# Another common order, engine choices and PSUM banks for the same operations in a four-block attention kernel

## The chip, the cores and the metric

The kernel runs on one core of a Trainium2 chip. The metric is the device time of one execution in microseconds (us), taken as the median of several runs. Before the change it is 410.13 us.

## The reference

Four residual blocks follow each other on an input `x` of 2048 tokens by 512 features, in bfloat16, two of kind A (linear attention) and two of kind B (attention to the last 256 tokens), all with 32 heads of 16 features:

```python
def _A_ref(x, wqkv, wo):
    ...
    phi = lambda t: jnp.where(t > 0, t + 1, jnp.exp(t)) + 1e-6
    pq, pk = phi(q), phi(k)
    kv = jnp.einsum("bhsd,bhse->bhde", pk, v)
    z = jnp.einsum("bhsd->bhd", pk)
    num = jnp.einsum("bhqd,bhde->bhqe", pq, kv)
    den = jnp.einsum("bhqd,bhd->bhq", pq, z)[..., None] + 1e-6
    o = num / den
    return (...) @ wo

def _B_ref(x, wqkv, wo):
    ...
    mask = (idx[:, None] - idx[None, :] >= 0) & (idx[:, None] - idx[None, :] < W)
    p = _softmax(jnp.where(mask, scores, -1e9), axis=-1)
    o = jnp.einsum("bhqk,bhkd->bhqd", p, v)
    return (...) @ wo

x = x + _A_ref(_layernorm(x), A_wqkv, A_wo)
x = x + _B_ref(_layernorm(x), B_wqkv, B_wo)
x = x + _A_ref(_layernorm(x), A_wqkv, A_wo)
x = x + _B_ref(_layernorm(x), B_wqkv, B_wo)
```

## The kernel before

The tokens are cut into 16 tiles of 128. The residual stream stays in SBUF (`xres`) throughout. The class `Plan` first writes down some 2,500 operations as a graph, each with the engines it may run on, what it reads and writes, and the PSUM tiles it uses. Nothing is scheduled on the chip: `place()` unpacks a table of bytes, `TABLE`, and takes four things from it: one common order of all operations, the engine of each, the PSUM bank (one of eight) of each PSUM tile, and which of an operation's waits stands first. Each engine then runs its operations in that common order, and `synchronise()` adds the semaphore waits that data and banks need. A PSUM bank goes to its next tile only when all users of the tile before are done, so the banks set waits too.

The work falls into three stretches:

- **Keys of the first A block** (to about 50 us). For each tile: mean and variance of the row (`stats` L382, `aggr` L383 on DVE), a power on POOL (`pow` L384), the normalised row (`xn` L385), a transpose (L391 by DMA, or L397 on PE with a copy L404), key and query projections (L420, L434), and `phi` from an exponential on ACT (L443) and VectorE work (L444, L448, L450). Sums over tokens gather in PSUM (L501).
- **First middle stretch** (about 50 to 250 us): for each token tile the end of block A, block B, and the keys, queries and values of the second A block. Denominators of the A block come for four tiles together: a matmul group `den` (L563), a reciprocal (L567), its copy `recb` (L568), a spreading matmul group `spread` (L576), and one multiply per tile, `pqd` (L583 on DVE), after which `aout` (L420, `ps<-M,XQ`) multiplies by the folded output weights and `res` (L594) adds to the residual.
- **Second middle stretch** (about 250 to 409 us): the same A end and B block for the last two blocks.

Inside block B, for a token tile `j`: projections of queries and keys `bq` and `bk` (L434, `ps<-xT,wBp`, 16 matmuls a tile each) and values `bv` (L420, `ps<-wBv,xT`); copies out of PSUM `bqe` and `bve` (L409) and `bke` (ACT L615 or DVE L616), each on ACT or DVE as the table says; two DMAs from SP for the keys (`kd`, L624, `kB<-vp`) and two for the values (`vd`, L643), which rearrange them. Then score matmuls `s` (L667, and L709 or L712 for the far edge), exponentials `ex` on ACT (L677 and L722), masks on DVE or POOL (`mk`, L687 or L686, and L736 or L733; `mf`, L745 or L744), products with the values `pv` and `pw` (L768, L780), a reciprocal and a multiply on DVE (`rcp` L790, `div` L791), a DMA transpose `oT` (L391, `oT<-o`), the output projection `bout` (L420, `ps<-wBo,oT`), and again `res` (L594). In the second stretch rows of the result go out by a DMA from SP or POOL (L891). The staging area of the keys is cleared beforehand by ACT (L863) or POOL (L861).

The reading of the table, in `place()`:

```python
    order = [ops[raw[2 * k] + 256 * raw[2 * k + 1]] for k in range(n)]
    ...
        o.eng = ("PE", "ACT", "DVE", "POOL", "SP")[raw[2 * n + o.i]]
    ...
        x.banks = [raw[3 * n + k]]
    ...
        o.first = raw[3 * n + len(tiles) + o.i]
```

Of the kernel before, what the change touches and what calls it, by code (L numbers as in the profile page):

```python
# [900 lines left out]


TABLE = (
    r"c-p;M1-Kly&b4Gow!_TK%*@Qp%*@Qp%*@Qp%*@Qp427iJf99rrZQ3O7Chhy@?(WRm($Ue8?3v9MRMAxoRZvA%g;W#;N~x&osY|O0t8^;8DxzYlqN<pB<}#=!",
# [3 lines left out]
    r"N)ddm%BuD%GYnPL)E#wN?NVn|Lsd?7R2>w<H|n0s0-e;iDufa!3hkl1Dyb5~8)YB~M1bn>Ksm4w1d2gv^;VTpXH-&123a9F)PQUd5hB45RYBcXVN?qEUIl~V",
    r"Fib^;C=eA&KuL%Or64=xfbUdJ$OSQ=1Js0CP#S7OP>2pGp$yc8+)x(kKs~4r%^{Qur<y?{6;^eGRFDTcLpi9f8bC|v11+GU>I*AWD`*XEV5Mpc{a~u<1QFCU",
    r"wMwl~tJPYyTZL3zpesyQGgUX}4l~p&)dTjZ{?HS8!8tVm210K*ubQYqa6!$3`LGHGLtV817D9bhPpyVEP+MJ6d({D01a(w+6&%*WR@esXpoUru4b&3Yr!K04",  # L910
    r"@KCLXnyQw1q?STswO?(35b%Rq1_#u3xU8PSHCPUh)pghbPt=cU4n$H<)e1NSH((<?Q#&Cf?1IA(3XZ^0_(=_cl`s^Zfx=(ZEeH+6U@q*2O#pZko&(}=*bF1!",
    r"Hr#>Jum?uN7GOLB$6zFkf{5xBoQ1n!Q1Au3hTwP{_QF2+3PR%7a34ZoD0~SI;34dX(AWlJLR)+UVbEbLI0uA3tFU+vEC#`7*bcvepr|n%K7r`?Ewsm9RTPYh",
    r"9q<IafnfL}#D?<_2TsB%hzmbK42+FM@G)F~)c7;R#5h<Kb7L_qj<GNgUW5Xe2K!(kEQoKRBj&}vm=;T5VJwN4U<~Ai?;sz<#qXgL_QO(G8uLRLjE7^P9HxdJ",
    r"pa2wvvX~Fc<1Y{&6JQ$XjA>yY4#ujO5UXK2sE+BO2G+zxH~<IXNF0rq;aA9pS6~R%!CF`w>tc8uh5a!CX2<S02CqUy?14G3Cl1BLm;_0)u7~MxIPS&tI1Dpj",
    r"B#ew>aUYJyao7+VL4FjyACuw;%!rMlJ~qG!SOF_yCQOFOu?aMVF4z?t;tZ^WhcE>m!I^j%yWuoEiqml%q{LL13v=Qz?2RXI7S6`GI0p~lJlughu?il?@sJs_",
    r";4VCfli?IjfJsmpv*Kx7i|cSAoWbk39yj1Qyn*GR7gm68@LOzz8}TH*!LxWCH{k`mh!r8YzKJ1qV+^62U?r#wx3DSR#yfZy!|Tm>4<qVdQRxVJK019Lw_s3h",
    r"bu&z_gXj!;0fJtL8TBHZh*MxHgwmaL7d;6>>#aB$w_zk5R(I78a4{~y{Q44x(FJrcJr%d(6ugWD^;?Xg!|5w{6*K9Wx`Z}5mX59C==l0OjH~xxNnJ$8)7P++",
    r"PM`<tqI!rfrpxH1_z;KcY4AP%fRFGo?#AZW0?X>+x}2_{3+r6EB|gEYsC6r>sas=tom<z^c{J*Ty0q@5pJ63kQIF7>b!A;!*U`)HM;xw4=`p&l&Z4vGk-C8{",
    r"q{rz*I<c;&8|wNxi5{zy>d5*hjH-XeDEc{$*2^)v?x%mj2|AnZuP5r``h*^!8|f)JnO=b_agv^<PwM2lyH26A>odBCo~(1|srsyLtjFsnI;U=`qv`4ToPL3;",
    r"aIT)Go9Ui9pI(g@bYA@uFX@Z=yl$>v;e35aFVHD<3%v$g>MDAnKCEA3Rs9uK(_iBfy;P^ty>x1QMK98e^)TIA_t9x|XgZ>=>8m=ePN%0s80xEM!VNtGs_U>+",  # L920
    r"Lod@ebt?@t3uXh-cCBfko}q8)9eSr;u2<+;dZpf_@95q7wqB(l>PLE}zN_cx{4_{Mp?i9d-m7Qp0(4y;)vI+>YOUMoXcUZsQ$dPAA?UHbtlR3-Iubq6Pjx%p",
    r"UdNz_RGyycHTr>$NiXzEeM*O?3Uo|A*KsHoRiwxik783?8caiIC?%&VL=>G;P<%>C$tWc;6{3B*8r7hxl#0?&O`1$oC^hZZ;pml4OSPy0HKNKSG?g0C0sUHk",
    r"r45CobaYVHp|5pyDn;MuZ}l4;ib~U3U6<-neQHUCsR+%WS=5TslcizQnAYiWG@fSCeO-n!&;*)8Z*?Vd6oiJ;TpB?cDJa#ZqV%1fN0}%y6{9SafLc=<YD*m`",
    r"5iOyFw2azOR%%ZjX(?^dTlF@*UeBkIG@CZ)je3*btea3Lnnq{nEPb!f(GNN?HKPSomVVK{>Lk>Z7SbYGPHU+%t)o$-=tq5#E>jn}M2l%X{iJ`^8>lO7q^s0|",
    r"u2E3lLYrta6{qVool4MFx=Z&d7+;}oRFcZkXc|NJC^+Aw<}{YF(Q&##w`d~WrtXxTdQcAPNe}1*J)@iyio@_Wx<eNz7lr2Y^qfvoZrV=0XcC3x9rS`;(oPD;",
    r"5%?A5<ku9QzoxG!7f0f6NH`?t=3NwmBeUVQyn=R<<tW^ads9R{MJuTft)jj(fCkbYipK5vG!3E?{4Jg2ew2q|@EVHF{ple+qP%p9-_T=vOZn(K`krEOY>vtC",
    r"IS41<y>y!6a8xeDXZQ*i;nnnnp7RU7%1@~<|3Hq<az1{^3He9*iC%GjPQ(TH8Ykwj_%#>fuemtyqhx%9lJn10l#}pLIz~ykgYKwHa6vA`-*5_!$CbGXm*Gx&",
    r"KOLZN`3-mD(p-|Oa#=n|)%Xw{rXJj#dvbNI#hv&fr{vlkms4>b?#x}d2G`_%e2G)@0RDw~@n!DHX}CZ4<__G42eD@2Uuhr@=CrJsc>$;6bKI8~@(^Cc<+u*#",
    r"<qCYBfy*;;U9QLVc_<I#;XHyb@JO!6qj(O_<)8RxzRvS_1<&UOe1mWDExyfnxFg@?RlJgy@IAiI4|p**<c5--mvSXu!;N??|H8krlF_`3$M9HQ&g*zRKjaL&",
    r"n#b{YZp;&S15f15ypc0<Cf>rCc@w|oMzWQ+aTCtMS@{uX<4HW3xAP9p&LB<sJ8s6UI0x_KUHm=o<~_WZMfP!XZp|$ir46^_AK1tgp2|P6mi>Hy4>Czmna0zZ",  # L930
    r"Wd;Y6nLLZF9OXlNn2)fN;Bt&-^J6~FPxvW6;}8;3!b=dzAq6G76q4LhSn^9=$s;+XfE1CU5<zlFC@CiSq_ISlCQ?G0N@!^>VWfi$m*Ub}`baZrE-@vnbd(m-",
    r"QbtHCX)T?kvqX`ovPQy5G+8TMB$9NMZqir!Nq^}s(Iu7)kaaRr21;aUBW<Of#FmmWSLVrlDJ6sCplpysQd(ljC>bn^WU(xfGSWj9%3+BkJ!OGZkn++?M#~T>",
    r"CqreJ9Fz63OqR=W86ztsu9TIHa#F_1CRr&bWV39MNitcc$SJubQ{}Y0lq)h#rpr-zC9fr(T$cE<R1!!+87F5Xp-E)6$|^Z4S7p4MlSDE>CdyaxwUF5+*CeCK",
    r"WD=VhvPamQm+K-XiP<YhB(u37Gv&5qH5Da=?30V~jieM~oY^ir<c?GlYi>wVb64(3D*08s2Yz#39!V$@+RT#KvRWQU7L!^Y%R{Lw-%1*JBXcB-`9Xe^AZDQn",
    r"Yl51eB$!DoNhG{UDvL~T6Vfa;kxdknOfpGkc_PV7a-&UD6T)OOXp&0=lSOt)4zo+LN;tDyqM2+G-NZ84O->WT#5A!@F0)_Kn6&1t6f)n*0ZC`Rm)z#56gEXn",
    r"QPa}oG5O3h$!l)PbNNMDnI@*SX=j?6IHtXcYx0|0Qr!G39ZW&f%)F3dCZ368;+wLjfQe{In=&Sa>1aBe5~iFfZ#tPurh@5ZdYj6oqN!rqm_DY8RF#w_l}T-?",
    r"Nf%RHx|yz~rpaJxNG;Rf)HV}McT>kqGLubRGsT=V>CGwA!t^jJO;0n&Of{=bKU2@NHK)y7)7K0%X=RmJX41)WQ{SvG4a@*D&)hV(%x$yDq?Zgb%~Um;O><+c",
    r"wOh;rlTp@~LB`o?rn(ty)|s_tx~VC(B#6Cdg4#1?h`Dbbn4xBvS#LI)vu3z?Wj2^m=8BnNN||%!wHaYXnjPk<sV$?;dGnQ-ZyK71=9<}R9-A?ykqKrSn=m%4",
    r"-EAJ3aQ2DWW44=Zrli?xo|%1Sr+IEJnEmFd32qOW>t?JuY+jlo_JBEP#+er;nvG$L+VN(lnPsBe8>X23#>BKG?Gh8)UNo1?*Cv*oZ4%jCCW*alYM6-jTl3aL",
    r"vTw{?Q_3DOOU+S}*haQ->@jo4gtw*b_vQx^&&IXG>~Zs>8DW1i$?eZ(xQ%Z^*rZn3KK2&__E*!_Ca~pf1RK>Rw8?C0+s{_8X>B^2!dA538MIMs8e86`x0!5Z",  # L940
    r"o7q;f8Ei(I($=!6Y)Bi**0Hs1SzAX2+AMaEtt&ZgE*show)LcntuHI>PTN4L+1xgd&1+ZL)pn$<YCGCaw!W=rN89SQvmIq?*nBp>En|1tthTPrW+&O2_Mz=!",
    r"yV^&#v7KVG+XA+M-EH^T5_YofW*^%owyB+9n%M((zwK^|+cCDeePSC~ZP(bfcAOn+Ti8~%r6t?iuCoU%+r##R*<!caf_A*^VW-+c_Nm=w580k}f}L)M+Glp6",
    r"J!J>jY4)`3WzX0dwy>RLzp_K@dfVTAZQIy}wzoZEkJ+R4oIP*n+Mn!m`;DD#=h%7nXZwpiZs*%Y_N_f(x7)?`J8Rtnd(yVG?W}V_+y%SPUbWxbU+p#9-k!CW",
# [172 lines left out]
```

## Time and profile before

| | us |
|---|---|
| three runs | 409.38, 410.13, 411.01 |
| median | 410.13 |
| the profiled execution, its own time | 411.18 |
| its span in the trace | 409.45 |
| granted TensorE clock | 1.00 of full speed |

Engines are PE (TensorE matmul), PEld (its weight loads), DVE (VectorE), ACT (ScalarE), POOL (GpSimd) and SP (SyncE, which issues DMAs). A row of the table of groups names line, engine, operation, `out<-in`, the shapes and the count, then busy time and mean duration, then the idle time just before them and what ended it. A row of the waits reads: who waited, for whom, us in total, times, longest. In a row of the timeline the first number is the start, the second the length, and a bracket gives the idle time before it and its releaser. Busy time of PE counts overlapping matmuls once.

### The profile page before, as it was taken

To read this page: it belongs to the slowest core of one execution; us is meant where nothing else is said; L and a number is where in the kernel's file an instruction comes from. 1 tells how busy PE (TensorE), PEld (TensorE's weight loads), DVE (VectorE), ACT (ScalarE), POOL (GpSimd) and SP (SyncE) were. 2 spreads that over 40 slices of the span, in tenths; PEclk is the share of its full clock that TensorE was granted. 3 is DMA by queue.
4 is the path that set the end of the run, shared out by engine and by line. 5 is a ranking of instruction groups with operands and counts; after the bars stand their busy time and mean duration, and the time that the engine had idled before them with its cause. 6 is when DMAs were issued, how large, how long until landed. Compare 5 with 4: busy or idle time off the path is not lost.

```text
span 409.5 us, 18147 instructions
## 1 busy us (share of the span) xinstructions
PE 382.0 (93%) x7918; PEld 257.4 (63%) x7995; DVE 319.7 (78%) x720; ACT 355.3 (87%) x462; POOL 158.2 (39%) x263
## 2 busy tenths in 40 slices
PE   8999999999989999999999999899899999989786
PEld 3554776667656556575558667577657666656554
DVE  6986899887888888887875899797787579645476
ACT  3796899999999999999996355789999899999992
POOL 3552331345355344233344201130374635545442
PEclk9999999999999999999999999999999999999999
DMA  7557128443425435553251101434233433463252
GB/s 228 156 121 178 54 53 160 107 68 82 94 72 116 92 72 108 101 100 83 52 83 29 27 2 29 108 70 115 50 102 96 108 82 85 115 126 82 69 134 79
DMA packets 67286, 37.75 MB, mean 92 GB/s; under 512 B 47880, under 2 KB 62344, under 8 KB 67208
## 3 DMA queue, kind: packets, MB, share of 16 engines
q1 hardware_dynamic: 66816, 35.54, 38.5%
q8 instruction: 63, 1.03, 1.1%
q0 software_dynamic: 384, 1.05, 0.7%
q14 instruction: 15, 0.12, 0.2%
q10 hardware_dynamic: 8, 0.00, 0.0%
HBM read 6.29 MB, written 2.10 MB: 20 GB/s over the span
## 4 chain that ended last, share of the span: by engine, by line
PE 57%; ACT 28%; DVE 9%; issue 3%; DMA 2%; SPq 1%
PE ps L420 19%; ACT pb L677 16%; PE ps L434 13%; PE ps L768 8%; PE ps L667 6%; ACT pb L722 4%; ACT vp L677 4%; PE ps L501 3%; PE ps L780 3%; DVE stats L382 1%; PE ps L712 1%; DVE xres L594 1%; DMA wA<-in_A_wqkv_dram 1%; ACT tE L443 1%; DVE XQ L450 1%
## 5 line engine op out<-in xcount | busy, mean ns | idle before, releaser
L677 ACT ACTIVATE pb<-ps 128x1024 bf16<-128x1024 f32 (+3 forms) x224 | 198.4, 980 | 8.7 <-PE ps L667 7.7
L384 POOL TENSOR_TENSOR rs<-mv,negh 128x1 f32<-128x1 f32 x64 | 36.8, 575 | 85.6 <-DVE mv L383 83.6
L434 PE MATMUL ps<-xT,wBp 128*128 128x128 bf16 x1024 | 68.4, 219 | 1.2 <-ACT pb L677 0.6
L434 PEld LDWEIGHTS ps<-xT,wBp 128*128 128x128 bf16 x1024 | 58.7, 98 | 11.8 <-issue 3.3
L768 PEld LDWEIGHTS ps<-vB,pb 128*128 128x128 bf16 x1712 | 54.3, 96 | 10.9 <-issue 4.7
L768 PE MATMUL ps<-vB,pb 128*128 128x52 bf16 (+1 forms) x1712 | 59.7, 184 | 0.4 <-DVE XQ L409 0.2
L686 POOL TENSOR_SCALAR_AFFINE_SELECT pb<-pb 128x512 bf16<-128x512 bf16 x46 | 31.3, 681 | 62.2 <-ACT pb L677 27.8
L667 PE MATMUL ps<-XQ,kB 32*128 32x256 bf16 (+2 forms) x1024 | 48.3, 262 | 5.7 <-DMA kB<-vp 1.7
L722 ACT ACTIVATE pb<-ps 128x1024 bf16<-128x1024 f32 x50 | 48.5, 1033 | 3.4 <-PE ps L712 2.4
L594 DVE TENSOR_TENSOR xres<-ps,xres 128x512 bf16<-128x512 f32 x63 | 43.1, 684 | 9.9 <-PE ps L420 9.3
L443 ACT ACTIVATE tE<-ps 128x512 bf16<-128x512 f32 x64 | 38.5, 612 | 13.6 <-PE ps L420 7.3
L420 PE MATMUL ps<-wA,XQ 128*128 128x512 bf16 x173 | 45.7, 379 | 2.8 <-issue 0.8
L382 DVE BATCH_NORM_STATS2 stats<-xres 128x6 f32<-128x512 bf16 x64 | 43.2, 679 | 3.1 <-DMA xres<-in_A_x_dram 2.5
L744 POOL TENSOR_SCALAR_AFFINE_SELECT pb<-pb 128x1024 bf16<-128x1024 bf16 x30 | 34.5, 1149 | 24.0 <-DVE tE L444 10.1
L733 POOL TENSOR_SCALAR_AFFINE_SELECT pb<-pb 128x256 bf16<-128x256 bf16 x58 | 25.7, 467 | 41.6 <-DVE pb L736 14.8
L434 PE MATMUL ps<-XQ,wA 128*128 128x128 bf16 x512 | 35.7, 219 | 0.0
L667 PEld LDWEIGHTS ps<-XQ,kB 32*128 32x128 bf16 x1024 | 15.3, 92 | 32.1 <-ACT pb L677 11.3
L434 PEld LDWEIGHTS ps<-XQ,wA 128*128 128x128 bf16 x512 | 30.8, 98 | 6.6 <-issue 0.6
L420 PE MATMUL ps<-wBv,xT 128*128 128x512 bf16 x105 | 29.4, 380 | 4.9 <-ACT pb L677 2.1
L420 PE MATMUL ps<-wBo,oT 128*128 128x512 bf16 x108 | 29.9, 380 | 2.5 <-issue 1.4
L420 PE MATMUL ps<-M,XQ 128*128 128x512 bf16 x113 | 30.0, 380 | 2.1 <-issue 0.8
L790 DVE RECIPROCAL rc<-ps 128x16 f32<-128x16 f32 x64 | 13.9, 238 | 21.6 <-PE ps L780 21.1
(128 smaller groups left out, 600.1 us busy)
## 6 DMA issues: line engine op xcount, KB each, us to landing
vB<-vS SPq DMA_DIRECT2D x64, 136.0 KB, 2.7
kB<-vp SPq DMA_DIRECT2D x64, 128.0 KB, 2.4
xres<-in_A_x_dram SPq DMA_DIRECT2D x6, 256.0 KB, 4.1
wA<-in_A_wqkv_dram SPq DMA_DIRECT2D x4, 256.0 KB, 3.5
pb<-in_B_wqkv_dram SPq DMA_DIRECT2D x4, 256.0 KB, 4.0
out_dram<-xres POOLq DMA_DIRECT2D x8, 128.0 KB, 2.4
out_dram<-xres SPq DMA_DIRECT2D x7, 128.0 KB, 2.2
...
```

The lines of the kernel that those rows point to most:

```text
L382: self.on("DVE", "stats", lambda e: e.bn_stats(K.stats[:, t % 8, 0:6], K.xres[:, t, :]), key, dve(512), rd=[("xres", t)], wr=[("stats", t ...
L384: self.pow = self.on("POOL", "pow", lambda e: e.tensor_tensor(K.rs[:, t, :], K.mv[:, t, 1:2], K.negh[:], ALU.pow), key + 0.03, (640, 690), ...
L420: m = e.matmul(K.ps(ps), lhs(c), rhs(c), start=c == 0, stop=c == 3)
L434: m = e.matmul(K.ps(ps)[:, f * P:(f + 1) * P], w(c, f), xT(c), start=c == 0, stop=c == 3)
L443: self.on("ACT", "E", lambda e: e.activation(K.tE[:, s, :], K.ps(ps), ACT.Exp, bias=0.0), key, act(512), wr=[("tE", s)], ps=[ps])
L594: self.on("DVE", "res", lambda e: e.tensor_tensor(K.xres[:, t, :], K.ps(po), K.xres[:, t, :], ALU.add), key, dve(512), rd=[("xres", t)], w ...
L667: m = e.matmul(K.ps(two(gq // 2)[gq % 2])[:, ns * i:ns * i + ns], K.kB[rows, j % 4, 2 * f + b, :, :], K.XQ[rows, f, q:q + ns], start=True, ...
L677: return e.activation(out(h, ns).rearrange("p (f g) c -> p f g c", f=n), i, ACT.Exp, bias=0.0, scale=0.25)
L686: return e.affine_select(out=x, in_=x, compare_op=ALU.is_ge, fill=0.0, base=1, pattern=[[0, 4 * n], [2, 64]], channel_multiplier=-1)
L722: return e.activation(o.rearrange("p (f g) b c -> p f g b c", g=2), i, ACT.Exp, bias=0.0, scale=0.25)
L744: return e.affine_select(out=x, in_=x, compare_op=ALU.is_ge, fill=0.0, base=-2, pattern=[[0, 16], [-2, 64]], channel_multiplier=1)
L768: m = e.matmul(K.ps(ps[f // 2])[:, cols(f, gq, wide(f, gq))], stat(b, f, gq)[:, c:c + P], vals(b, f, gq, wide(f, gq)), start=f % 2 == 0 an ...
```

## The change

Only the bytes of `TABLE` change; the operations, their instructions and their data are the same. Of the four things in it:

- the common order is another permutation;
- 2,542 operations keep their engine except 109, counted from the two orders: 28 `mk` and 13 `mf` go from POOL to DVE and 18 `mk` and 17 `mf` from DVE to POOL; `bke` 3 from DVE to ACT; `bqe` 4 from ACT to DVE; `bve` one each way; `Me` 2 from DVE to ACT; two clears (one of L359/L361, one of L861/L863) from POOL to ACT; `wp` (L374) 2 from ACT to POOL; `ve` 2 each way; `ge` one each way; `recb` 2 from ACT to DVE and 1 back; `oTe` 2 from DVE to ACT and 1 back; and of the 15 whole-row result DMAs 6 go from SP to POOL and 2 from POOL to SP. By count ACT gets one operation more, DVE five more, POOL two fewer, SP four fewer;
- most PSUM tiles get another bank;
- the waits that stand first change with the order.

```diff
 TABLE = (
-    r"c-p;M1-Kly&b4Gow!_TK%*@Qp%*@Qp%*@Qp%*@Qp427iJf99rrZQ3O7Chhy@?(WRm($Ue8?3v9MRMAxoRZvA%g;W#;N~x&osY|O0t8^;8DxzYlqN<pB<}#=!",
+    r"c-p;J1)$wF&y{3Lw#&@S%*@Qp%*@Qp%*@Qp%*@Qp++jQJpS-vIYqxf5yY0(;_u6r!Bb_6~$s;HT(IEyDf@lyKqQEnU5ETH@LOM`T7#Iu`f%H%mVnSJn1;ro(",
...
 )
```

Three places of the order matter below.

**Start of the second middle stretch, on PE.** `ps<-xT,wBp` are query and key projections of 16 matmuls each, `ps<-wBv,xT` values, `L397` transposes, `L563` and `L576` the denominators. Before:

```order
L434 MATMUL ps<-xT,wBp 128x128 x16
L563 MATMUL ps<-ones,eps 32x128 x4
L563 MATMUL ps<-XQ,zs 32x128 x16
L434 MATMUL ps<-xT,wBp 128x128 x16
L397 MATMUL ps<-ident,xn 128x128 x4
L420 MATMUL ps<-wBv,xT 128x512 x4
L434 MATMUL ps<-xT,wBp 128x128 x16
L576 MATMUL ps<-rec,spread 128x128 x16
L434 MATMUL ps<-xT,wBp 128x128 x32
L667 MATMUL ps<-XQ,kB 128x224 x8
```

After:

```order
L434 MATMUL ps<-xT,wBp 128x128 x32
L397 MATMUL ps<-ident,xn 128x128 x4
L420 MATMUL ps<-wBv,xT 128x512 x4
L563 MATMUL ps<-ones,eps 32x128 x4
L563 MATMUL ps<-XQ,zs 32x128 x16
L397 MATMUL ps<-ident,xn 128x128 x4
L420 MATMUL ps<-wBv,xT 128x512 x4
L434 MATMUL ps<-xT,wBp 128x128 x16
L576 MATMUL ps<-rec,spread 128x128 x16
L434 MATMUL ps<-xT,wBp 128x128 x32
L667 MATMUL ps<-XQ,kB 128x224 x8
```

The rows don't tell queries from keys: before, the first 16 are tile 0's queries and the second 16 (behind `L563`) its keys; after, the keys are the first 16 of the 32 and the queries the rest. So the keys now stand further ahead of the first score matmul (`L667`).

**The same place on ACT.** `L615` copies the keys of a tile out of PSUM, `L409` queries (`XQ`) or values (`vS`), `L443` is an exponential of block A, `L404` a transposed tile. Before:

```order
L409 ACTIVATE vS<-ps 128x32x16
L409 ACTIVATE XQ<-ps 128x4x128
L443 ACTIVATE tE<-ps 128x512
L615 ACTIVATE vp<-ps 128x512
L404 ACTIVATE xT<-ps 128x512
L615 ACTIVATE vp<-ps 128x512
```

After:

```order
L863 ACTIVATE vp<-zc 128x1152
L404 ACTIVATE xT<-ps 128x512
L615 ACTIVATE vp<-ps 128x512
L443 ACTIVATE tE<-ps 128x512
L404 ACTIVATE xT<-ps 128x512
L409 ACTIVATE XQ<-ps 128x4x128
```

The first key copy now stands behind a transposed tile and a clear (`L863`), and ahead of the first query and value copies.

**Between the values of tile 9 and its output projection, first middle stretch, on PE.** `L780` ends the values of a tile, `ps<-wBo,oT` is the output projection. Before:

```order
L780 MATMUL ps<-vB,pb 64x34 x32
L667 MATMUL ps<-XQ,kB 128x256 x8
L420 MATMUL ps<-wA,XQ 128x512 x8
L709 MATMUL ps<-XQ,kB 128x64 x32
L420 MATMUL ps<-wBv,xT 128x512 x4
L420 MATMUL ps<-wA,XQ 128x512 x4
L667 MATMUL ps<-XQ,kB 128x256 x8
L420 MATMUL ps<-wA,XQ 128x512 x4
L768 MATMUL ps<-vB,pb 128x52 x16
L420 MATMUL ps<-wBo,oT 128x512 x2
```

After:

```order
L780 MATMUL ps<-vB,pb 64x34 x32
L420 MATMUL ps<-wA,XQ 128x512 x8
L709 MATMUL ps<-XQ,kB 128x64 x32
L420 MATMUL ps<-wA,XQ 128x512 x4
L420 MATMUL ps<-wBv,xT 128x512 x4
L667 MATMUL ps<-XQ,kB 128x256 x8
L420 MATMUL ps<-wA,XQ 128x512 x2
L420 MATMUL ps<-wBo,oT 128x512 x4
```

One score group, two key or value matmuls and a value group less stand between the two.

**Third group of four denominators in the second middle stretch, on PE.** `L576` spreads the reciprocals, `ps<-M,XQ` uses tiles that DVE multiplied by them. Before:

```order
L712 MATMUL ps<-XQ,kB 64x64 x64
L576 MATMUL ps<-rec,spread 128x128 x16
L434 MATMUL ps<-xT,wBp 128x128 x16
L667 MATMUL ps<-XQ,kB 128x224 x8
L420 MATMUL ps<-M,XQ 128x512 x6
```

After:

```order
L712 MATMUL ps<-XQ,kB 64x64 x64
L434 MATMUL ps<-xT,wBp 128x128 x16
L576 MATMUL ps<-rec,spread 128x128 x16
L667 MATMUL ps<-XQ,kB 128x224 x8
L420 MATMUL ps<-M,XQ 128x512 x8
```

The query projection of 16 matmuls moved from behind the spreading to ahead of it.

More of the change, by code (lines that the diff above doesn't have):

```diff
@@ L908 @@
[L908 to L943, printed above, removed]
@@ new lines @@
+    r"bcWdQ)Wv}=@Z4$02*Y6nWP&HoLRT0GO(8DCgKm%+nn8S+4c(y<2=stakN`%*7{~$+=0HM740B-}tcRX34-P^v7z-O9Hw1+|Fb=XpBG?E?AUkA(<d6cI!+Zz=",
+    r"<)9^8fwqtXlEHIm2Zx|H^nt063l2jIC=V&26;y?Im<l#Q8+ZY!Auq(o{16PL!4b#@S78D4g?^9}aspr)2!jiuH4K2z&>zOb1egeuU^67ZMKBrK!%?^f*C8R^",
+    r"fDW((I>HvH4KJY@d;tStF(3|tFQF3<Cc>?-6sABGYzSeXI)ugPunkIq!tJmO3P1*&3CAEDR>i?^9KvHp)OZt4z%6Kp%b^e!#%eeezJeWa5>7!TybWK&X$TIP",
+    r"aTk08)v-NBz_YLu&OmV}0gOfP72E;AyKoQgLl#Vo58zvP4Ri22h=@fo5+*@|4rf43h>SJRVh~J<Q85Z8$E;WkLqInC9)e;ptclSu24=^cSQ$b>aV&wQAsObt",
@@ new lines @@
+    r"xtIb=Vl7OCxiC7G!rE8{N<tnijVZA%hJ)N#2J2uwEQbxS1vY|NPz73IS*(xEumi4u3eXXoV=HWpZLl5;fd&v3+G2gE2%%sl41><t2RmU8Tm@^OC-%jNup0Vd",
+    r"H|&MApb2!r-LMw=;~waW=U@O1#O^o<YrtUajptz=?uGdn34VZ8xBxFecz6gGVIl5=)wl>3<0DvuKf)!50GDA2?uV^-0DgjPxD=P+FR&K3;}AT6>+m2phM~9~",
+    r"AHy(w3LEe#)`dg31E1kFypB6@7v8|(I1-=Za$JEU@Ch8oFYrs;h|gdp2FD|K6hmN0+=RFAHtxnz_!S<*&A0_a;T^n-b>JqB#yxl%&mhxT1PYCYkcjr;*BG4k",
+    r";c?uLLJ#mEzQ9NL4StIuDKv$kHq@40qNcDEhGJqUx{p7@8wf{^f>IEQh3zOBS!z$OFgl&UlNgN7;VFzlu`v$b!yoY{e1cIaF8+)~C<b+)^B9vZU~I}wu}D!K",
@@ L960 @@
+    r"(8l7U5PMPtbcH9a59PO=59lWwQ1-wi{Ptl9Y(5Ie*U!~Q32bik>*P14j~Q4*Z!`gq)n9wy*U{g91idbSzdP_xllQJ6zBT@K^4oQUzmN0bXzw?G&o%gv7yca-",
+    r"enhx`1>_%c`7HLo4FNA;zfSOTK>kq%zs>1m00XYmTPJTh1W@>-l<@r{evl%*r-kqn<#-Puz9*M|TGUUj75)be_`X{VKY;^&s^bTp|H>Udud5N?ZN-nS5dJND",
+    r"{G>X(ZAtjQ+)nTVMaGW`j{oLPhM$9p|5o(>UA&LKS@E-)`ZKe|4?j}>E{#tLi62_V|FVGi&il?kE-Zee8Xu|LUkCp`sV_2%",
 )
```

63 lines of the change are left out of this document (44 added, 19 removed).

## The prediction

> **What bounds the kernel now.** I read the page first (busy time, then the chain that ended last), then the engines' busy time by stretches, then PE's waits, then the timeline at the places where the order changes. The page:
>
> ```profile
> span 409.5 us, 18147 instructions
> PE 382.0 (93%) x7918; PEld 257.4 (63%) x7995; DVE 319.7 (78%) x720; ACT 355.3 (87%) x462; POOL 158.2 (39%) x263
> PEclk9999999999999999999999999999999999999999
> PE 57%; ACT 28%; DVE 9%; issue 3%; DMA 2%; SPq 1%
> ```
>
> PE is busy 93% at an undisturbed clock and carries 57% of the chain; ACT carries 28%. So 409.5 - 382.0 = 27.5 us of PE idle is all that another order can win, since it takes no PE work away. By stretches:
>
> ```profile
> core 0: us, PE busy (x) PEld busy (x) DVE busy (x) ACT busy (x) POOL busy (x), PEclk, DMA share, GB/s
> 0.00:10.00 10.00, 8.05 (x39) 3.31 (x39) 6.33 (x18) 3.77 (x6) 3.92 (x14) 1.00 0.72 224
> ...
> 250.00:260.00 10.00, 8.20 (x157) 6.93 (x156) 8.63 (x19) 6.65 (x11) 1.10 (x2) 1.00 0.35 97
> ...
> 345.00:396.00 51.00, 44.43 (x1284) 31.03 (x1290) 30.29 (x66) 49.40 (x60) 25.16 (x46) 1.00 0.45 100
> 396.00:409.40 13.40, 9.61 (x247) 6.88 (x248) 8.15 (x21) 5.35 (x11) 3.51 (x6) 1.00 0.36 105
> ```
>
> Idle on PE: 1.95 us in the head, 1.8 at the start of the second middle stretch, 51.0 - 44.4 = 6.6 between 345 and 396 and 3.8 in the last 13.4. The rest, 27.5 - 14.15 = 13.4, lies thinly over some 325 us. Between 345 and 396 ACT is busy 49.4 of 51: there the exponentials set the pace, and an order of PE can do nothing about it. PE's waits:
>
> ```profile
> PE ps L420 <- issue: 5.1, 32, 0.2
> PE ps L420 <- ACT pb L677: 2.1, 4, 0.7
> PE ps L667 <- DMA kB<-vp: 1.7, 1, 1.7
> PE ps L667 <- ACT pb L677: 1.4, 3, 0.6
> PE ps L780 <- issue: 0.7, 1, 0.7
> PE ps L667 <- issue: 0.7, 1, 0.7
> PE ps L420 <- DMA wA<-in_A_wqkv_dram: 0.5, 1, 0.5
> ```
>
> The largest single one, 1.7 us, is for the DMA that lays out the first keys of the second middle stretch. The 5.1 us of `issue` are 32 turns of 0.16 us, a price that each turn pays in any order.
>
> **The change part by part.** The sum is made against the profiled execution, 411.18 us (span 409.45 and 1.73 around it); it was 1.05 us above the median of the runs.
>
> *A, the start of the second middle stretch.* PE's timeline, then ACT, the queue and the chain, then the landings of all key DMAs (minimum, median, maximum):
>
> ```profile
> 251.77 1.07 PE L434 MATMUL ps<-xT,wBp 128*128 128x128 bf16 x16
> 252.68 0.39 PE L397 MATMUL ps<-ident,xn 128*128 128x128 bf16 x4
> 253.12 0.81 PE L420 MATMUL ps<-wBv,xT 128*128 128x512 bf16 x3
> 253.76 1.06 PE L434 MATMUL ps<-xT,wBp 128*128 128x128 bf16 x16
> 254.75 0.40 PE L576 MATMUL ps<-rec,spread 32*128 32x128 bf16 x16
> 255.09 1.96 PE L434 MATMUL ps<-xT,wBp 128*128 128x128 bf16 x32
> 258.79 0.37 PE L667 MATMUL ps<-XQ,kB 32*128 32x224 bf16 x8 [1.75 <-DMA kB<-vp]
> ```
>
> ```profile
> 253.36 0.74 ACT L615 ACTIVATE vp<-ps 128x512 bf16<-128x512 f32 x1
> ```
>
> ```profile
> 254.13 1.14 SPq L624 DMA_DIRECT2D kB<-vp  x2
> ```
>
> ```profile
> 254.67 4.08 DMA kB<-vp
> ```
>
> ```profile
> DMA to landing us min/median/max: 1.9/2.4/4.3
> ```
>
> Tile 0's keys end at 252.84 on PE, ACT copies them, SP issues at 254.13, and the second of its two DMAs lands 4.08 us after 254.67, at 258.75. From the keys to the score matmul that is 5.9 us. PE had 4.2 us to fill it with, the rows from 252.68 to 257.05, and then stood still. In the new order the keys are the first 16 of the 32 matmuls, and behind them come: the second 16 (0.9, about half of 1.96), a transpose (about 0.25 net, since rows overlap), values (0.85), `L563` (about 0.4), another transpose and values (1.1), 16 matmuls (0.9), `L576` (0.35) and 32 (1.8): 6.5 us against the 5.9 that the same chain of copy, issue and landing needs. So the wait of 1.7 goes, by 0.6 us. What is late next is a query copy of tile 1 (`L409`), which the last 32 matmuls give about 0.3 us to spare. On ACT the key copy now stands behind a transposed tile and a clear; the clear is only in the way if it has not run by then, and ACT was idle 3.35 of these 10 us. Bounds: -1.7 when the landing is as slow as here; 0 when it is the median, 2.4, since then the score matmul would have waited for nothing in the old order either. I take -1.7: all other rows around it are steady, and the landing belongs to this place.
>
> *B, tile 9.* The values end, DVE divides, SP transposes by DMA, and `bout` waits for that:
>
> ```profile
> 166.16 0.68 PE L780 MATMUL ps<-vB,pb 128*64 128x34 bf16 x32
> ...
> 167.59 1.67 PE L420 MATMUL ps<-wA,XQ 128*128 128x512 bf16 x7 [0.41 <-ACT pb L722]
> ...
> 172.99 0.59 PE L420 MATMUL ps<-wBo,oT 128*128 128x512 bf16 x2
> ```
>
> ```profile
> 167.69 0.75 DVE L791 TENSOR_TENSOR o<-ps,rc 128x256 bf16<-128x256 f32 x2
> ```
>
> ```profile
> DMA to landing us min/median/max: 2.4/2.6/5.2
> ```
>
> The distance from the end of `L780` (166.8) to `bout` was 6.2 us. A 512-column matmul costs (1.67 - 0.38)/6 = 0.215 us in a row of its kind. The new order has 18 of them (3.9), the narrow edge `L709` (0.35) and one score group (0.33): 4.6 us. The chain needs 168.44 - 166.8 = 1.65 to the end of the divide and 2.6 for the median transpose, 4.25. It fits by 0.35; with the slowest landing on record, 5.2, it costs 2.25. Bounds 0 and +2.25; I take +0.2, near the median.
>
> *C, the third denominators.* PE, then DVE:
>
> ```profile
> 294.14 0.40 PE L576 MATMUL ps<-rec,spread 32*128 32x128 bf16 x16 [0.51 <-DVE o L791]
> 294.78 1.07 PE L434 MATMUL ps<-xT,wBp 128*128 128x128 bf16 x16 [0.23 <-ACT vp L722]
> ```
>
> ```profile
> 294.60 2.48 DVE L583 TENSOR_TENSOR XQ<-ps,XQ 128x512 bf16<-128x512 f32 x4 [0.51 <-PE ps L576]
> ```
>
> The query projection now runs ahead of the spreading, so it covers the 0.51 us that the spreading waited for DVE, and its own 0.23 for a bank may go. In exchange it no longer covers the first of DVE's four multiplies, 2.48/4 = 0.62 and about 0.1 to start: only a score group (0.33) stands before `ps<-M,XQ`, so a new wait of 0.4 arises. -0.51 - 0.23 + 0.4 = -0.3, bounds -0.7 (no new wait) and +0.7 (both old ones stay in another place and the query copy goes ahead of the multiplies).
>
> *D, the other order and banks.* Of the waits for ACT on `L420`, 2.1 us in four, 0.7 lies behind 345 us, where the rows on ACT are the same in both kernels; 1.4 stands at places that are re-dealt. I take half of it as gone, -0.7, a choice and no derivation: a new place can also wait, so the bounds are -1.4 and +1.4. The two odd gaps of 0.7 (`issue`, in the middle of a group) follow no semaphore and are kept.
>
> *E, engine choices.* PE's load is the same. ACT takes over two clears and loses shorter copies, and has one operation more:
>
> ```profile
> L863 ACT ACTIVATE vp<-zc 128x1152 bf16<-128x1152 bf16 x2 | 2.3, 1158 | 0.1
> ```
>
> Two clears of 1.16 in place of two copies of 0.74 and one operation more of at most 1.16 make at most +2.0 us of ACT load. The swaps stand before 345, where ACT has idle time (3.35 us in 250 to 260 alone) and PE sets the pace: I take 0, bound +2.0, reached if PE always waits for ACT there. The head keeps its order up to the weights' DMA (0.5 us) and counts 0, as does the tail.
>
> Sum: -1.7 + 0.2 - 0.3 - 0.7 = -2.5, so 408.7 on the profiled execution's scale and, less 1.05, **407.6 us**. Its own range, from A at 0 (+1.7) and C and D at their better and worse halves (about 1 each way), is 406.5 to 409.6. A difference of 0.5% (2.05 us) is about what a measurement of this kernel tells from no change.
>
> **The rivals.**
>
> *The key wait is no feature of the kernel.* The landing of 4.08 us is near the slowest of its kind (4.3). If it is an accident of the profiled execution, which was 1.05 above the median, the other runs have no such wait, and only B to D are left: 410.13 - 0.8 = 409.3. For it: the median landing of 2.4. Against it: the slow one comes where two key DMAs are issued back to back, which happens there in each execution.
>
> *PE's thin idle time falls broadly.* The 13.4 us beside the named places shrink by a third: -4.5 more, 403.1. For it: banks and order are new nearly everywhere. Against it: 5.1 us of it are turns of 0.16 that stay. Beside the row of 0.215 us per matmul, which leaves nothing between neighbours inside a run of matmuls, stands a rule of the Trainium skill ("Perfetto Trace Analysis", section "Identifying the Most-Contended Engine"): busy matmul time is not a good measure of how near TensorE is to its limit, and the busy share of weight loads is. By that rule the 63% here would leave over a third of the span, an estimate of some 150 us; the trace does not agree that an order could reach it, since the matmuls stand end to end.
>
> *VectorE and GpSimd stretch each other's masks onto PE's path.* In the trace some of DVE's operations last far over their median (minimum, median, maximum):
>
> ```profile
> L385 DVE TENSOR_SCALAR xn<-xres,mv,rs x48: 371/406/1333, 51.8 to 351.5; 128x512 bf16<-128x512 bf16 x48
> L687 DVE TENSOR_TENSOR pb<-pb,tri x22: 380/418/964, 66.4 to 397.6; 128x512 bf16<-128x512 bf16 x22
> ```
>
> Up to 1333 - 406 = 0.93 and 964 - 418 = 0.55 us. The change hands 41 masks to DVE and 35 to POOL, so which of them run together is dealt anew. With ten more stretches of 0.55 straight ahead of a PE wait the time is 407.6 + 5.5 = 413.1; from nine on (412.5) it is slower beyond what a measurement tells. Against it: PE's waits name no mask on DVE among their larger ones, DVE has 9% of the chain, and the count of masks on DVE rises by only six. The Trainium skill ("SBUF — State Buffer", section "SBUF: two separate sides") speaks for the mechanism: GpSimd and a VectorE operation with two SBUF inputs take a shared pair of ports as an exclusive lock for a whole instruction, and the other is blocked. The trace agrees as far as the 964 ns row goes; that GpSimd was the cause it does not show.
>
> *Tile 9 pays the slow transpose.* B at its upper bound: 407.6 + 2.05 = 409.65, no difference to tell. For it: the margin is 0.35 us. Against it: half of the landings are at or under 2.6.
>
> **How the numbers follow.** Forecast .46, no real key wait .17, broad fall .13, stretched masks .15, tile 9 .09. Faster by over 0.5% is below 408.1: two thirds of the forecast's own range (.31) and the broad fall (.13), .44. Slower, above 412.2: .15. The rest, .41, lies within. The range leaves out most of the stretched masks and half of the broad fall, 403.6 to 412.0.
>
> **What would show it.** In the new profile the wait of the first `L667` for `kB<-vp` near 258 is gone (A), the first `bout` behind tile 9 shows no wait over 0.3 for a DMA (B), a wait of some 0.4 for `XQ L583` stands at the third group while `L576` has none (C), and PE's idle time is about 25 us. I am wrong if the score matmul there waits for the DMA again, if PE's idle time in 345 to 396 has changed by over 1 us, or if DVE masks appear among PE's larger waits.

## The result, and the profile after

The changed kernel takes 407.5 us (median of 4 runs, 407.19 to 407.93), the kernel before 410.35 (4 runs beside it). The ratio is 0.9925, interval 0.9898 to 0.9953: 2.85 us less, faster by 0.7%. Forecast were 407.6 us and 2.5 less. (The count of moved engine choices in the section on the change should read 111, the sum of its own list.)

Lines of the page of the kernel after, then PE and the other engines in two stretches of the same kind as before:

```profile
span 405.5 us, 18118 instructions
PE 382.4 (94%) x7923; PEld 258.1 (64%) x7995; DVE 317.5 (78%) x725; ACT 355.4 (88%) x463; POOL 156.0 (38%) x253
```

```profile
250.00:260.00 10.00, 9.79 (x206) 6.79 (x206) 9.67 (x22) 8.88 (x15) 1.72 (x3) 1.00 0.35 96
...
345.00:392.00 47.00, 41.20 (x1227) 29.37 (x1235) 29.00 (x66) 46.35 (x56) 23.19 (x36) 1.00 0.44 101
```

By these pages PE's busy time is what it was (382.4 against 382.0), and its idle time fell from 27.5 to 23.1 us. From 250 to 260 only 0.2 us of idle time are left of 1.8. From 345 to 392, 47.0 - 41.2 = 5.8 us are idle, where the kernel before had 6.6 up to 396.

Both idle times are too large, though. Of the 7,995 matmuls, which the weight loads count, the traces lack the records of 77 before and of 72 after, nearly all of them 512-column matmuls on `L420`, and a missing record looks like idle time. The second profile of the kernel before (below) has them all:

```profile
PE 392.2 (96%) x7995; PEld 257.8 (63%) x7995; DVE 319.9 (78%) x720; ACT 355.0 (87%) x462; POOL 158.0 (39%) x263
```

There PE is idle for 408.1 - 392.2 = 15.9 us, and the row of 32 turns of `issue` does not exist; nor does it in any other profile that has all its matmuls. So the prediction's "price that each turn pays" was missing records, and its 27.5 us to win were some 16. Spans and starts of instructions are not touched by this.

PE's waits in the kernel after:

```profile
PE ps L420 <- issue: 5.1, 32, 0.2
PE ps L420 <- ACT pb L677: 2.8, 5, 0.7
```

The wait of 1.7 us for `kB<-vp` is gone, and so are the two gaps of 0.7 us (`issue`) on `L780` and `L667`. The start of the second middle stretch on PE, and the queue:

```profile
253.59 0.40 PE L576 MATMUL ps<-rec,spread 32*128 32x128 bf16 x16
253.93 1.96 PE L434 MATMUL ps<-xT,wBp 128*128 128x128 bf16 x32
255.82 0.37 PE L667 MATMUL ps<-XQ,kB 32*128 32x224 bf16 x8
```

```profile
250.00 1.14 SPq L624 DMA_DIRECT2D kB<-vp  x2
```

The first score matmul follows the projections with no bracket. But tile 0's two key DMAs did not take 4 us any more: they landed 2.0 and 2.1 us after their issue, the second at 252.61, 3.2 us before PE asked for them.

That score matmul is a good landmark, since it begins the same work in every kernel here. The profiled pair differs by 409.5 - 405.5 = 4.0 us: 258.79 - 255.82 = 3.0 ahead of it (1.75 of them the wait), and 150.7 - 149.7 = 1.0 behind it, where the two gaps of 0.7 were.

### The profile page after: what moved, and what is told of

Read it like the earlier page. It is cut to its first block, busy times and chain, and to the rows that moved or that the text cites. A ratio compares the mean times of both kernels' runs of the same rounds, so it can differ in the third digit from the quotient of the medians.

```text
span 405.5 us, 18118 instructions
## 1 busy us (share of the span) xinstructions
PE 382.4 (94%) x7923; PEld 258.1 (64%) x7995; DVE 317.5 (78%) x725; ACT 355.4 (88%) x463; POOL 156.0 (38%) x253
## 4 chain that ended last, share of the span: by engine, by line
PE 61%; ACT 31%; DVE 3%; issue 2%; DMA 1%; SPq 1%
PE ps L420 22%; ACT pb L677 19%; PE ps L434 15%; PE ps L768 6%; PE ps L667 5%; ACT pb L722 5%; ACT vp L677 3%; PE ps L780 3%; PE ps L501 2%; PE ps L712 2%; ACT tE L443 2%; DMA wA<-in_A_wqkv_dram 1%; PE ps L476 1%; ACT vp L722 1%; PE ps L709 1%
## 5 line engine op out<-in xcount | busy, mean ns | idle before, releaser
L677 ACT ACTIVATE pb<-ps 128x1024 bf16<-128x1024 f32 (+4 forms) x224 | 197.5, 985 | 6.0 <-PE ps L667 5.2
L384 POOL TENSOR_TENSOR rs<-mv,negh 128x1 f32<-128x1 f32 x64 | 37.8, 590 | 89.3 <-DVE mv L383 87.3
L744 POOL TENSOR_SCALAR_AFFINE_SELECT pb<-pb 128x1024 bf16<-128x1024 bf16 x35 | 40.3, 1150 | 33.0 <-DVE tE L444 14.1
L667 PE MATMUL ps<-XQ,kB 32*128 32x256 bf16 (+2 forms) x1024 | 48.1, 262 | 3.1 <-ACT pb L722 0.8
L686 POOL TENSOR_SCALAR_AFFINE_SELECT pb<-pb 128x512 bf16<-128x512 bf16 x43 | 29.3, 680 | 50.7 <-ACT pb L677 33.7
L420 PE MATMUL ps<-wA,XQ 128*128 128x512 bf16 x180 | 46.8, 380 | 1.9 <-issue 1.1
L443 ACT ACTIVATE tE<-ps 128x512 bf16<-128x512 f32 x64 | 38.3, 613 | 9.1 <-PE ps L420 3.5
L420 PE MATMUL ps<-wBv,xT 128*128 128x512 bf16 x110 | 30.5, 380 | 3.3 <-issue 1.3
L420 PE MATMUL ps<-wBo,oT 128*128 128x512 bf16 x105 | 29.1, 380 | 4.2 <-ACT pb L677 1.7
L667 PEld LDWEIGHTS ps<-XQ,kB 32*128 32x128 bf16 x1024 | 15.3, 92 | 27.1 <-ACT pb L677 9.0
L420 PE MATMUL ps<-M,XQ 128*128 128x512 bf16 x111 | 30.2, 380 | 2.2 <-issue 1.1
L733 POOL TENSOR_SCALAR_AFFINE_SELECT pb<-pb 128x256 bf16<-128x256 bf16 x44 | 18.8, 451 | 27.6 <-ACT pb L677 12.0
```

Source lines behind the costliest of these rows:

```text
L384: self.pow = self.on("POOL", "pow", lambda e: e.tensor_tensor(K.rs[:, t, :], K.mv[:, t, 1:2], K.negh[:], ALU.pow), key + 0.03, (640, 690), ...
L420: m = e.matmul(K.ps(ps), lhs(c), rhs(c), start=c == 0, stop=c == 3)
L443: self.on("ACT", "E", lambda e: e.activation(K.tE[:, s, :], K.ps(ps), ACT.Exp, bias=0.0), key, act(512), wr=[("tE", s)], ps=[ps])
L667: m = e.matmul(K.ps(two(gq // 2)[gq % 2])[:, ns * i:ns * i + ns], K.kB[rows, j % 4, 2 * f + b, :, :], K.XQ[rows, f, q:q + ns], start=True, ...
L677: return e.activation(out(h, ns).rearrange("p (f g) c -> p f g c", f=n), i, ACT.Exp, bias=0.0, scale=0.25)
L686: return e.affine_select(out=x, in_=x, compare_op=ALU.is_ge, fill=0.0, base=1, pattern=[[0, 4 * n], [2, 64]], channel_multiplier=-1)
```

## The experiments

The theory was the prediction's: the kernel before waits 1.7 us for the keys in each execution, and the new order removes that. The first rival was that the late landing is an accident. A third theory came up on the way, that PE's own instructions arrive late.

### The kernel before, a second profile

No edit.

> The kernel before, unchanged, in a second profiled execution. If the key wait belongs to the place (theory of the prediction): PE waits 1.2 to 2 us for kB<-vp at the first L667 near 258 us again, and the key DMA lands there after about 4 us. If the slow landing was an accident of the one execution (rival): that wait is under 0.3 us, the landing is near the median of 2.4, and the span is some 1.5 us shorter. The two gaps of 0.7 us near 380 and 386 (issue): at the same two instructions if they belong to the program, elsewhere or absent if not.

One time of 409.92 us, span 408.1. The chain at the landmark, and PE's longest waits:

```profile
254.29 3.90 DMA kB<-vp
258.19 0.05 issue
258.24 0.37 PE ps L667 x8
```

```profile
PE ps L420 <- ACT pb L677: 2.2, 6, 0.5
PE ps L667 <- DMA kB<-vp: 1.6, 1, 1.6
```

The wait came again, 1.6 us, with a landing of 3.90: no accident of the one execution. The two gaps of 0.7 did not come again, though the prediction had kept them as a fixed part.

### The keys of tile 0 moved, alone

```diff
 L434 MATMUL ps<-XQ,wA 128x128 x8
-L434 MATMUL ps<-xT,wBp 128x128 x16
+L434 MATMUL ps<-xT,wBp 128x128 x32
 L563 MATMUL ps<-ones,eps 32x128 x4
 L563 MATMUL ps<-XQ,zs 32x128 x16
-L434 MATMUL ps<-xT,wBp 128x128 x16
 L397 MATMUL ps<-ident,xn 128x128 x4
```

> The kernel before with one part of the change alone: tile 0's key projection, its copy and its two DMAs stand ahead of its query projection at the start of the second middle stretch. The keys come about 1.3 us earlier on PE (one group of 16 matmuls and the denominators). Theory of the prediction: most of the 1.7 us wait goes, 1.2 to 1.7 us, to about 408.8. Rival (the wait is an accident): no change, within 0.3 us of the kernel before.

409.24 us against 410.74, ratio 0.9963 (0.9937 to 0.9988): 1.5 us less, as forecast. The score matmul starts at 257.01 and waits for nothing:

```profile
255.11 1.96 PE L434 MATMUL ps<-xT,wBp 128*128 128x128 bf16 x32
257.01 0.37 PE L667 MATMUL ps<-XQ,kB 32*128 32x224 bf16 x8
```

Term A is real and has its size (by the interval, anything from 0.5 to 2.6 us). Both 0.7 gaps were in this profile again.

### The kernel after with the keys put back

```diff
-L434 MATMUL ps<-xT,wBp 128x128 x32
+L434 MATMUL ps<-xT,wBp 128x128 x16
 L397 MATMUL ps<-ident,xn 128x128 x4
 L420 MATMUL ps<-wBv,xT 128x512 x4
 L563 MATMUL ps<-ones,eps 32x128 x4
 L563 MATMUL ps<-XQ,zs 32x128 x16
+L434 MATMUL ps<-xT,wBp 128x128 x16
 L397 MATMUL ps<-ident,xn 128x128 x4
```

> The kernel after with the keys of that tile put back behind the denominators, so that PE has 4.1 us of work between them and the score matmul as before, in place of 6.5. Theory of the prediction (landing of about 4 us at this place): a wait of 1.5 to 2.5 us for kB<-vp is back and the time rises by that, to about 409.3. Rival (an ordinary landing of 2.2 to 2.4): a wait of 0.2 to 0.8, time up by at most 0.8.

408.19 us, ratio to before 0.9938 (0.9914 to 0.9963), where the kernel after has 0.9925: some 0.7 us lost at most, inside the intervals of both.

```profile
254.16 1.96 PE L434 MATMUL ps<-xT,wBp 128*128 128x128 bf16 x32
256.05 0.37 PE L667 MATMUL ps<-XQ,kB 32*128 32x224 bf16 x8
```

(The bank of one PSUM tile of 1,002 differs too.) No wait for the keys came back. With the same 4.1 us of cover as before, an ordinary landing is early enough, and in the new surroundings it was ordinary, 2.06 us. So the landing of 4 us does not belong to this piece of order. Both readings of the place were too simple.

### Two splices

```diff
-common order, engines and banks of before
+late_after: before's first 1,540 operations, then the rest as in after
+early_after: after's first 1,548 operations, then the rest as in before
```

> The order, engines and banks of before up to about 238 us, those of after from there on. Against before, the two profiles lose 2.8 us of PE's idle time behind that point and 1.2 ahead of it. Theory of the prediction (most of the gain is the start of the second middle stretch and what follows): 1.7 to 2.8 us faster than before, about 407.8. Rival (the gain lies spread over the whole kernel, and the key wait is an accident): about half of the gain, 1.2 us, about 409.1.

410.31 us, ratio 0.9993 (0.9975 to 1.0012): no gain, against both theories. Its score matmul starts at 256.57 with no wait, 2.2 us earlier than in before, but the rest then takes 408.2 - 256.57 = 151.6 us and not 149.7. One place stands out on PE:

```profile
341.45 0.36 PE L667 MATMUL ps<-XQ,kB 32*128 32x224 bf16 x6
342.78 0.27 PE L667 MATMUL ps<-XQ,kB 32*128 32x224 bf16 x2 [0.97 <-issue]
```

In the middle of a group of eight matmuls PE stands still for 1 us and no semaphore is involved: the same kind of gap as the two in before. It accounts for about half of the 1.9 us. The kernel after runs these operations in the same order without it.

> The order, engines and banks of after up to about 240 us, those of before from there on. Theory of the prediction (small waits re-dealt): the first 240 us give 1.2 us less idle time on PE, and the key wait of the second middle stretch stays, so 0.8 to 1.3 us faster than before, about 409.6. Rival (only the start of the second middle stretch matters): no change.

408.54 us, ratio 0.9958 (0.993 to 0.9985): 2.2 us faster, where 0.8 to 1.3 were expected, because this kernel, with before's order at the landmark, has no key wait:

```profile
254.84 1.84 PE L434 MATMUL ps<-xT,wBp 128*128 128x128 bf16 x30
256.61 0.37 PE L667 MATMUL ps<-XQ,kB 32*128 32x224 bf16 x8
```

What delays the keys is seen in the DMA view: a packet of instructions. In before, the window in which they should have landed, 256.5 to 257.6, holds one instruction packet:

```profile
q8 instruction: 1, 0.02, 5.4%
```

By the packets of the trace it runs from 256.56 to 257.52, and the last key packet lands 1.2 us after it ends, at 258.75. In the second profile of before it runs from 256.00 to 256.96, and the landing is at 258.19, again 1.2 us after. In early_after the keys have landed at 256.35, and the packet starts at 256.61. It is a meeting of two transfers, missed by 0.3 us. The data transfers around the keys were the same there as in the second profile of before: SP issued them at 253.75, 254.93 and 255.57 or 255.58 in both.

The traces bear this out well beyond the one place. Over all 14 profiles, 329 key DMAs had an instruction packet in flight 1.3 to 2.1 us after their issue; they landed after 3.2 us (median). The other 553 landed after 2.05. In the first profile of before alone these are 25 DMAs with 3.2 and 39 with 2.1, so a late landing is nothing rare; it costs time only where PE comes for the keys before it.

### Shifting PE's instructions

The page gives the instruction packets of the kernel before:

```profile
q8 instruction: 63, 1.03, 1.1%
```

63 packets of 16 KB are PE's program: the trace has 16,240 instructions of PE, and at 64 bytes each they fill 63.4 of them. All weight loads have a row in the traces, 7,995 in the kernel before, so each gap can be counted out in the program. Over all runs but the one with changed engines, 23 intervals of over 0.32 us from the start of one weight load to the start of the next, with no wait between them, stand at the same place of every 256 instructions, the 193rd or 194th counted from PE's first row:

```
kernel: interval in ns (which 256)
before 892 (58), 933 (59)        before_again 331 (39)
swap_keys 887 (58), 930 (59)     early_after 886 (12)     late_after 1311 (50)
before_shift 558 (44), 585 (49)  after_232 465 (63)       late_232 1124 (51)
after_shift 443 (41), 522 (44), 827 (49), 668 (52), 405 (60), 1445 (61)
late_shift 591 (44), 466 (49), 1545 (61), 1433 (62)
undo_start 325 (44), 458 (45)
```

Others are one of 0.52 us at `L563` in the kernels that begin with after's order, and the paces of long matmuls in the first 8 us and, in two shifted kernels, the last 15. The kernel after and before_232 have none at that place. In 22 of the 23 a packet had ended 1.25 to 1.6 us before PE went on (the one of before_again is an ordinary pace: 278 ns in before). And at none of the 874 such boundaries in the 14 profiles did PE go on sooner than 1.18 us after the end of a packet. That is what one expects if PE waits for the packet. The two of undo_start make 0.8 us, about what it loses behind the landmark: 406.4 - 256.05 = 150.4 against 149.7. The Trainium skill ("Runtime: NRT & Kernel Launch", section "Instruction fetch mechanics") says that an engine's instructions are refilled in blocks of 16 KiB, 256 instructions, and that crossing a block is mostly hidden. The traces agree with the block, and with "mostly": 22 of the 874 crossings show a gap. But in late_shift four of them make some 3 us. The test was to move all of PE's instructions by a part of a block, in the warm-up where the head waits anyway:

```diff
-for _ in range(9):
-    e.matmul(self.PS[:, SPARE, :], warm[:, 0:P], warm, start=True, stop=True)
+for _ in range(5):
+    e.matmul(self.PS[:, SPARE, :], warm[:, 0:P], warm, start=True, stop=True)
+for _ in range(64):
+    e.matmul(self.PS[:, SPARE, 0:16], warm[:, 0:P], warm[:, 0:16], start=True, stop=True)
```

> The kernel before with the same shift of PE's instructions by 60 matmuls at the head. Theory A (late instruction packets make gaps where they fall): the gaps of issue stand elsewhere, the time may move by up to 1.5 us either way, and the key wait near 258 us may change too. Theory B: 410.7 within 0.5 us, and the key wait of 1.6 stays.

> The kernel after with the same shift. Theory A: up to 1.5 us slower or no faster than 407.5, since its profile shows no long gap of issue to lose. Theory B: 407.5 within 0.5 us.

> The splice late_after, with 60 matmuls more in PE's warm-up at the head: five of 512 columns and 64 of 16 columns in place of nine of 512, about the same time, nothing else. The profile of late_after showed gaps of issue on PE near 343 us, about 2 us in all, that the kernel after does not have at the same operations. Theory A (the gap is PE's instructions arriving late: the instruction packets of 16 KB fall at other operations): the shift moves or removes the gap, and the time falls by 1 to 2 us, to about 408.6. Theory B (the gap belongs to the order of the work there): the time stays within 0.5 us of 410.3.

413.74, 412.35 and 413.4 us; ratios to before 1.0062 (1.003 to 1.0095), 1.0032 (1.0004 to 1.0059) and 1.0069 (1.0038 to 1.01). By the medians a shift of 120 instructions, half a block, costs the kernel after some 4.9 us and the kernel before 3.0, two or more times what theory A allowed; late_shift was to gain 1 to 2 us and lost 3. The gap of late_after moved to other operations, but more and longer ones came. The gaps in after_shift, then in late_shift:

```profile
PE ps L712 <- issue: 1.6, 4, 0.6
...
PE ps L780 <- issue: 1.2, 1, 1.2
```

```profile
PE ps L780 <- issue: 2.6, 2, 1.3
...
PE ps L712 <- issue: 0.6, 2, 0.4
```

They now stand in `L712` and `L780`, groups of 64 and 32 short matmuls, and at the same place of the block as all others. The landmark of before_shift, at 259.62, shows no wait for the keys either.

The gaps are not all of it. The profiled before_shift (411.62 us, the fastest of its ten) has two of 0.7 us in all, but PE waits there in five places, 2.8 us together, for DMAs that the kernel before does not wait for; the two largest rows:

```profile
PE ps L434 <- DMA xT<-xn: 1.0, 2, 0.7
PE ps L420 <- DMA oT<-o: 0.9, 1, 0.9
```

Each of the five DMAs met an instruction packet, 1.1 to 2.1 us after its issue, and landed after 3.8 to 4.4 us; late_shift has four more of the kind. What the other executions of before_shift, up to 416.8 us, add to this no profile shows.

The second shift was 232 instructions, nearly a whole block, chosen by the times of the weight loads so that hardly any block is run out in under 3.3 us (at the end one of 3.1 is left):

```diff
-for _ in range(9):
+for _ in range(1):
     e.matmul(self.PS[:, SPARE, :], warm[:, 0:P], warm, start=True, stop=True)
+for _ in range(124):
+    e.matmul(self.PS[:, SPARE, 0:16], warm[:, 0:P], warm[:, 0:16], start=True, stop=True)
```

> The kernel after with PE's warm-up made of one matmul of 512 columns and 124 of 16 in place of nine of 512: about the same time at the head, and all later instructions of PE stand 232 places further on, 24 short of the 256 that fill a packet of 16 KB. The gaps of issue in the profiles so far all stand at the same place of every 256 instructions. Theory A (the phase decides, since PE waits for its next packet only where short matmuls run out a packet in under some 3.3 us): 232 is nearly a whole turn, and by the times of the matmuls around the boundaries a good one, so 407.5 or up to 0.5 less, although more was inserted than in after_shift. Theory B (inserted instructions cost, or any shift disturbs): 412 or more.

> The kernel before with the same shift of 232 instructions. Theory A: no gaps of issue over 0.3 us, 409 to 410.5, and the key wait near 258 us gone or not by where the key DMA meets a packet. Theory B: 413 or more. What stays between this and after_232 is the order itself: by the prediction 2.5 us, by the rival that the gain is mostly the packets' phase under 1 us.

> The splice late_after (order of before to 238 us, of after from there) with the same shift of 232. Theory A: the gap of 1.3 us near 342 us and what it drags goes, 410.3 becomes 408 to 409. Theory B: 413 or more, as with late_shift.

408.95 us (ratio 0.9961, 0.994 to 0.9982), 409.06 (0.9975, 0.995 to 1.0) and 411.07 (1.001, 0.9992 to 1.0028). The phase decides, not the number of inserted instructions: twice as many cost the kernel after 3.4 us less. It is 1.45 above the unshifted kernel, where theory A had expected nothing or less; all of it lies ahead of the landmark (257.28 against 255.82); behind the landmark the two agree within 0.1 us (407.1 - 257.28 = 149.8). Before_232 has neither key wait nor gap:

```profile
255.81 1.84 PE L434 MATMUL ps<-xT,wBp 128*128 128x128 bf16 x30
257.58 0.37 PE L667 MATMUL ps<-XQ,kB 32*128 32x224 bf16 x8
```

At this phase the two orders take the same time, 409.06 and 408.95. But the head, which is the same in both orders, ran later in these two profiles, and not equally. PE's wait for the weights ends at 8.55 in after and at 8.60 in before; in after_232 and then in before_232:

```profile
9.92 1.04 PE L420 MATMUL ps<-wA,XQ 128*128 128x512 bf16 x4 [0.91 <-DMA wA<-in_A_wqkv_dram]
```

```profile
9.27 1.04 PE L420 MATMUL ps<-wA,XQ 128*128 128x512 bf16 x4 [0.64 <-DMA wA<-in_A_wqkv_dram]
```

From there to the end after_232 takes 397.2 us and before_232 397.7, unshifted 397.0 and 400.9. So in these profiles the phase of 232 saves the kernel before some 3 us behind the head and does nothing for the kernel after, and the new order stays ahead by about half a us.

Theory A missed with late_232: its gap came back at 344.7, on the next group and again at the 193rd of its block, and the expected 408 to 409 were not reached.

```profile
344.68 0.23 PE L768 MATMUL ps<-vB,pb 128*128 128x52 bf16 x2 [0.92 <-issue]
```

There the block before the gap was no fast one (7.2 us in late_after); its packet came late, 7 us after PE had passed the boundary where 2 are common. Why it was held back there in both splices, and not in the kernel after, stays open.

### The new order with the old engines

```diff
-engine choices of after
+engine choices of before, order and banks of after
```

> The kernel after with the engine choices of before, order and banks kept. By the prediction the engine choices are worth nothing (bound: before's ACT load is up to 2 us smaller): 407.5 within 0.7 us. Rival (the new engines belong to the new order): 1 to 3 us slower, since copies and masks wait in the wrong queues.

429.69 us, ratio 1.046 (1.0428 to 1.0492): 22 us slower than the kernel after. PE's longest waits, the stretch around the longest, and the page:

```profile
PE ps L667 <- DVE vp L450: 2.5, 1, 2.5
PE ps L420 <- DVE vp L409: 2.0, 2, 1.7
```

```profile
172.00:200.00 28.00, 24.97 (x439) 15.34 (x438) 18.70 (x42) 22.17 (x26) 6.87 (x10) 0.94 0.38 83
```

```profile
PE 397.3 (93%) x7995; PEld 259.7 (61%) x7995; DVE 318.0 (74%) x720; ACT 354.5 (83%) x462; POOL 156.1 (36%) x263
```

The engines' loads are the old ones, but copies and masks stand in queues that were ordered for other engines: waits of 0.8 to 2.5 us at some ten places, 428.6 - 397.3 = 31 us of idle time on PE, and in the stretch with the longest a granted clock of 0.94. This trace has all its matmuls, so it compares with undo_start, which has them too: 392.1 us busy and 14.3 idle. PE's busy time is 5 us longer for the same matmuls; in two stretches of 3.4 us, from 182.9 and from 421.8, the granted clock was 0.5, and the rest is not explained. The new order does not work with the old engine choices; the old order with the new choices was not run.

## Why the prediction was right, and where not

The time was right: 407.6 forecast, 407.5 measured. That it was right to 0.1 us is luck. On the scale of the profiled executions the forecast was 408.7, and the kernel after took 407.33: 1.4 us more went than the terms allowed, about the two gaps, and the 1.05 taken off for the median made up for most of it. Term by term, on the profiled pair (4.0 us of span):

- **A, -1.7: right in size and place.** The wait of 1.75 is gone; swap_keys alone gives 1.5 us. The step that failed is its reason, "the landing belongs to this place". The keys land late because one 16 KB packet of PE's instructions meets them; early_after, before_shift and before_232 have before's order there and no wait. The new order cures it twice over: the keys are 2.4 us better covered, and the meeting does not happen. The first rival ("no feature of the kernel") was wrong for before as it stands, where the wait came in both profiles.
- **B, +0.2: none came.** The output projection of tile 9 starts at once:

```profile
171.46 1.03 PE L420 MATMUL ps<-wBo,oT 128*128 128x512 bf16 x4
```

- **C, -0.3: about nothing, and by another wait.** From `L712` to the first recorded `ps<-M,XQ` it was 296.31 - 292.93 = 3.4 us in before (matmuls of the same kinds), and in after 293.18 - 289.86 = 3.3:

```profile
292.93 0.71 PE L712 MATMUL ps<-XQ,kB 32*64 32x64 bf16 x64
...
296.31 1.24 PE L420 MATMUL ps<-M,XQ 128*128 128x512 bf16 x5 [0.16 <-issue]
```

```profile
289.86 0.71 PE L712 MATMUL ps<-XQ,kB 32*64 32x64 bf16 x64
290.50 1.07 PE L434 MATMUL ps<-xT,wBp 128*128 128x128 bf16 x16
291.72 0.40 PE L576 MATMUL ps<-rec,spread 32*128 32x128 bf16 x16
292.63 0.37 PE L667 MATMUL ps<-XQ,kB 32*128 32x224 bf16 x8 [0.51 <-ACT vp L722]
293.18 1.67 PE L420 MATMUL ps<-M,XQ 128*128 128x512 bf16 x7 [0.18 <-issue]
```

  The old wait of 0.51 on `L576` went as forecast. In its place the score matmul waits 0.51 for ACT to free its bank, not `ps<-M,XQ` for DVE. The banks were not followed at this place.
- **D, -0.7: about -0.8 by what is left** of 4.0 when A, C and the two gaps are taken off, but not by the waits that the prediction named. Those for ACT on `L420` did not fall by half of 1.4: ahead of 345 us they fell from 1.4 to 0.4, and behind it, where the prediction kept them as they were, they rose from 0.7 to 2.4. Before and then after, from 345 us on:

```profile
PE ps L420 <- ACT pb L677: 0.7, 1, 0.7
```

```profile
PE ps L420 <- ACT pb L677: 2.4, 4, 0.7
```

  In all it is 2.8 us in place of 2.1. So the size of D came out by other waits; it was a choice, as the prediction says, and its size is luck. It lies ahead of the landmark (3.0 - 1.75 = 1.2 less) and is partly given back behind it.
- **The two gaps, "kept": wrong.** They are 1.35 us of the profiled difference, and the packets ahead of them ended 4.0 and 4.7 us after PE had passed the boundary, where 2 are common. They come in two of the three profiles with before's tail in its own phase (before and swap_keys; not before_again), and not in after.
- **E and the tail, 0.** The time behind the landmark, without the gaps, is within half a us. That the new engine choices cost nothing was true only as part of the new order.

The rival on the slower side did not show: no mask on DVE stands among PE's larger waits (the largest, for `L687`, is 0.2 us). The broad fall did not come either: beside A, C and the gaps only 0.8 us went.

What the prediction didn't see at all is that about as much hangs on the phase of PE's instruction packets as on the order: 3 to 5 us for half a block. So of the 4.0 us between the two profiles 3.1 are the key wait and the gaps, which hang on when a packet comes; what share of the 2.85 between the medians that is, two profiles of before and one of after can't tell, since the gaps come and go. How much the new order would keep in another phase, the runs bound only by the pair at 232 (0.1 us, or about 0.5 behind the head) and the pair at 120 (413.74 against 412.35, 1.4).
